# A 2x2 block product in seven multiplications inside a Fourier and feed-forward kernel

## The chip, the cores and the metric

One core of one Trainium2 chip. The time is the device time of one execution in microseconds, as the median of three runs. PE is the engine of the matrix products (PEld its weight loads), DVE, ACT and POOL are the vector, scalar and GpSimd engines, SP issues the transfers.

## The reference

```
x: (8, 3008, 256)
X  = rfft(x, axis=1)
Yr = Xr @ w_r - Xi @ w_i + b_r ;  Yi = Xr @ w_i + Xi @ w_r + b_i
Yr, Yi = sign(Y) * max(|Y| - 0.01, 0)
y  = irfft(Yr + i Yi)                        # (24064 tokens, 256)
h  = y @ w_in                                # 256 -> 2048
out = (h * clip(h + 3, 0, 6) / 6) @ w_out    # 2048 -> 256
```

All arrays are float32 except w_in and w_out, which arrive as float64.

## The kernel before

**Precision.** A float32 product is made of three single passes. Each operand is split into a high part and a low part (`split`, line 111: ACT copies the high part, DVE or POOL subtracts it for the low part), and `product` (line 116) sums low x high, high x low and high x high in PSUM. The weights of the feed-forward part are decoded on the chip from the 64-bit words (`decode`, line 135), in 16 bands of 512 columns: four of them with the buffers EARLY during the first batch's transform, the others with the buffers LATE during the first feed-forward units.

**Transform.** The length 3008 is 64 x 47, so the Fourier transform is one over n2 and one over n1. `stage1` (line 209) does the first for ten n1 at a time and writes to a scratch tensor in DRAM. `middle` (line 297) handles two k2 at a time, in three pieces: `s2` (over n1, with a split of the result), `s3` (the complex weights, the threshold, the rearrangement t, c, z, zhi, zlo) and `s5` (back over k1, to a second scratch tensor). `stage6` (line 413) goes back over k2 for one chunk of tokens, puts the features on the partitions and splits them into yhi and ylo, the low part on POOL.

**Feed-forward.** Each batch has seven chunks of tokens: four of 470 and three of 376 (MSPLIT). A unit is one chunk and 256 of the 2048 inner features, so a batch has 56 units and the whole run 448. `up` (line 451) makes 12 products into a PSUM tile ph of two banks (2 groups of 128 features x 2 halves of the 256 inputs x 3 passes), then on the whole tile: ACT relu(h + 3) into g, DVE min(g, 6) x h, ACT ghi, DVE glo. `down` (line 474) adds 12 products into po; it runs two units behind `up`.

**Order.** The main loop writes up(i), a slot, down(i - 2), a slot. The pieces of the transform of later batches lie in these slots: stage 2 to 5 of the next batch, stage 1 of the one after, stage 6 of the next chunk. The order of instructions on an engine follows this source order as far as operands are ready. Pools give two buffers to most tiles of the transform, three to ghi and glo; PSUM is ph (2 x 2 banks), po (2) and ps_a (2).

Of the kernel before, what the change touches and what calls it, by code (L numbers as in the profile page):

```python
# [37 lines left out]


def positions():  # L40
    """The order of the tokens in the result: by chunks, in each first n2 = q < 24, then n2 = 47 - q."""
    pos, order = sequence(), []
    for c, nj in enumerate(MSPLIT):
        n1 = 2 * sum(MSPLIT[:c]) + np.arange(2 * nj)
        order += [pos[n1, :NK].reshape(-1), pos[n1][:, N2 - np.arange(1, NK)].reshape(-1)]
    return np.concatenate(order)


def constants():
    """Matrices of the transforms, by shape alone."""  # L50
# [10 lines left out]
    # Sums of n2 = q and -q for the cosines, differences for the sines: rows (j, q), columns (c/s, j, k2),  # L61
    # and as the matrix is symmetric, rows (j, k2), columns (c/s, j, q) too.
# [4 lines left out]
    # rows (c/s, n1), columns k2, (re/im, k1)  # L67
# [5 lines left out]
    # rows (re/im, k1), columns (c/s, n1): for k2 = 0, then for the others  # L73
# [13 lines left out]
    f = lambda a, *s: np.ascontiguousarray(a.reshape(*s).astype(np.float32))  # noqa: E731  # L87
# [9 lines left out]
def spectral_ffn(ctx: ExitStack, tc: tile.TileContext, x, w_r, w_i, bias, w_in, w_out, f47, f64, g64, sgn, out):  # L97
    nc = tc.nc
    const = ctx.enter_context(tc.tile_pool(name="const", bufs=1))
    sb = ctx.enter_context(tc.tile_pool(name="sb", bufs=2))  # L100
    dram = ctx.enter_context(tc.tile_pool(name="dram", bufs=2, space=DRAM))
    ps_h = ctx.enter_context(tc.tile_pool(name="ps_h", bufs=2, space=PSUM))
    ps_o = ctx.enter_context(tc.tile_pool(name="ps_o", bufs=1, space=PSUM))
    ps_a = ctx.enter_context(tc.tile_pool(name="ps_a", bufs=2, space=PSUM))

    def room(wide=False):
        if wide:
            return ps_h.tile([P, 2, 512], F32, name="ph")[:, 0]
        return ps_a.tile([P, 512], F32, name="ps_a")

    def split(hi, lo, src, on=None):
        """src = hi + lo, each with the bits that one pass of a product carries."""
        nc.scalar.copy(out=hi, in_=src)  # L113
        (on or nc.vector).tensor_tensor(out=lo, in0=src, in1=hi.bitcast(F32), op=ALU.subtract)  # L114

    def product(ps, terms, start=True, stop=True):
        """The sum of (hi, lo)^T (hi, lo) over terms, into ps."""
        todo = [p for (ah, al), (bh, bl) in terms for p in ((al, bh), (ah, bl), (ah, bh))]
        for n, (a, b) in enumerate(todo):
            nc.tensor.matmul(out=ps, lhsT=a, rhs=b, start=start and n == 0, stop=stop and n == len(todo) - 1)  # L120

    def loaded(src, rows, cols, name, tag="g"):
        """A constant as its two parts."""
# [5 lines left out]

    depth = {"ghi": 3, "glo": 3, "ot": 1, "c": 1, "e": 1}  # L130

    def space(shape, dt, name, tag):
        return sb.tile(shape, dt, name=name, tag=tag, bufs=depth.get(tag, 2))

    def decode(src, hi, lo, cut, tags):
# [5 lines left out]
        e, m, r, mf, rf = (  # L141
            space([P, 2, 256], dt, t, tag) for t, dt, tag in zip("emrfg", (I32, I32, I32, F32, F32), tags[1:])
        )
# [5 lines left out]
        v.scalar_tensor_tensor(out=e, in0=high, scalar=-(1 << 31), in1=e, op0=ALU.bitwise_and, op1=ALU.bitwise_or)  # L149
# [3 lines left out]
        nc.gpsimd.tensor_tensor(out=cut(hi, 1), in0=mf, in1=base, op=ALU.mult)  # L153
# [3 lines left out]
        nc.gpsimd.tensor_tensor(out=cut(lo, 1), in0=rf, in1=base, op=ALU.mult)  # L157
# [8 lines left out]
    # brings the table of its functions in before the data is there  # L166
    nc.scalar.activation(out=three, in_=three, func=AF.Relu, scale=1.0)

    win_s = [const.tile([P, 2 * FF], F32R, name="w_in_" + t) for t in ("hi", "lo")]
    wout_s = [const.tile([P, NFT * D], F32R, name="w_out_" + t) for t in ("hi", "lo")]  # L170

    def in_band(f, early):
# [4 lines left out]
        decode(w_in, *win_s, cut, early)  # L177

    def out_band(f, early):
# [4 lines left out]
        decode(w_out, *wout_s, cut, early)  # L184

    EARLY = ("xin", "g", "yhi", "ylo", "qt", "ot")
    LATE = ("bt", "t", "Xhi", "zhi", "zlo", "Xlo")
# [19 lines left out]
    scr1, scr2, ys = {}, {}, {}  # L207

    def stage1(b):
        scr1[b] = dram.tile([2, N1, NK, D], F32, name="scr1")  # L210
        sets = [(n1, min(2 * J, N1 - n1)) for n1 in range(0, N1, 2 * J)]
        sets = sets[-1:] + sets[:-1]
        xins = {}

        def load(i):
            n1, n = sets[i]
            rows, w = (R47, 2 * D) if n == 2 * J else (n * NK, D)
            xins[i] = space([P, 2, 2 * D], F32, "xin", ("xin", "xin", "bt", "bt", "pt", "pt", "qt")[i] if b == 0 else "xin")
# [5 lines left out]
        if b == 0:  # L224
            shapes = [load(i) for i in range(len(sets))]
        for i, (n1, n) in enumerate(sets):
            rows, w = shapes[i] if b == 0 else load(i)
            xin = xins.pop(i)
            plus, minus = xin[:rows, 0, :w], xin[:rows, 1, :w]
            e = space([P, 2 * D], F32, "e", "t" if b == 0 else "e")[:rows, :w]  # L230
            (nc.vector if b == 0 else nc.gpsimd).tensor_tensor(out=e, in0=plus, in1=minus, op=ALU.add)
            (nc.vector if b == 0 and i % 2 else nc.gpsimd).tensor_tensor(out=plus, in0=plus, in1=minus, op=ALU.subtract)
            for c, src in enumerate((e, plus)):
                q = 2 * i + c
                tags = (("xhi", "xlo"), ("zhi", "zlo"), ("Xhi", "Xlo"))[q % 3 if b == 0 else 0]
                xs = [space([P, 2 * D], F32R, t, tag)[:rows, :w] for t, tag in zip(("xhi", "xlo"), tags)]
                split(*xs, src, nc.vector if b == 0 and (c == 0 or i % 2 == 0) else nc.gpsimd)
                ps = ps_o.tile([P, 2, 512], F32, name="po")[:, 0] if b == 1 and not ys else room(b == 0 and c)
                product(ps[:rows, :w], [([t[:rows, c * R47 : c * R47 + rows] for t in f47_s[:2]], xs)])
                a = space([P, 2 * D], F32, "a", ("a", "yhi", "ylo")[q % 3] if b == 0 else "a")[:rows, :w]  # L240
                if c and b == 0 and i in (0,2,4):
# [4 lines left out]
                nc.sync.dma_start(out=dst, in_=a.rearrange("p (g d) -> p g d", d=D))  # L246
                yield

    f64_s = const.tile([P, NK, P], F32, name="f64")
    sgn_s = const.tile([P, NK], F32, name="sgn")  # L250
    bias_s = const.tile([P, 2 * D], F32, name="bias")
    def load_f64(g):
        ks = slice(2 * g, 2 * g + 4)
        nc.sync.dma_start(out=f64_s[:, ks], in_=f64.rearrange("p (k c) -> p k c", c=P)[:, ks])

    w_m = [const.tile([P, 2 * D], F32R, name="w_m_" + t) for t in ("hi", "lo")]
    w_four = [[space([P, 2 * D], F32R, "w", tag) for _ in range(2)] for tag in ("ghi", "glo")]

    def weights():
        """w_i and -w_i, for batch 0; -(w_r + w_i) and w_i - w_r, for the others."""  # L260
# [18 lines left out]
    for i, _ in enumerate(stage1(0)):  # L279
        if i == 7:  # L280
            load_f64(0)
            r, k = [loaded(w, P, 2 * D, n) for w, n in ((w_r, "w_r"), (w_i, "w_i"))]
            nc.sync.dma_start(out=bias_s, in_=bias)
            nc.sync.dma_start(out=sgn_s, in_=sgn)
            g64_t = loaded(g64, P, 2 * P, "g64", "ot")
            todo = weights()
# [10 lines left out]
    def middle(b):  # L297
# [4 lines left out]
        bt, xs, zs, pt = {}, {}, {}, {}  # L302

        def s2(g):
            if g % 2 == 0:
                bt[g // 2] = sb.tile([P, 4, D], F32, name="bt")
                nc.sync.dma_start(out=bt[g // 2], in_=src[:, 2 * g : 2 * g + 4, :])
            if b == 0:
                if g and g % 2 == 0:
                    load_f64(g)  # L310
            ps = room(b == 0)
            psv = ps.rearrange("p (h r k c) -> p h r k c", h=2, r=2, k=2)
            for u in range(2):
                k2 = 2 * g + u
                for dh in range(2):
                    nc.tensor.matmul(  # L316
                        out=psv[:, dh, :, u, :],
                        lhsT=bt[g // 2][:, k2 % 4, dh * P : (dh + 1) * P],
                        rhs=f64_s[:, k2, :],
                        start=True,  # L320
                        stop=True,
                    )
            pv = ps.rearrange("p (h r c) -> p h r c", h=2, r=2)
# [218 lines left out]
    for i in range(len(units) + 2):  # L542
# [3 lines left out]
        if i >= 2:  # L546
            down(*units[i - 2])
# [50 lines left out]
```

## Time and profile before

| | |
|---|---|
| median of three runs | 2747.0 us (2746.18 to 2747.72) |
| span of the profiled execution | 2745.7 us |
| busy PE / PEld | 2678.2 us (98%) / 2495.5 us (91%), 15128 products |
| busy DVE | 1679.9 us (61%), 2439 instructions |
| busy ACT | 1329.7 us (48%), 1991 instructions |
| busy POOL | 473.4 us (17%), 349 instructions |
| mean granted TensorE clock | 0.986 |

The profile is of one execution, which has no time of its own beside its span from the first to the last instruction. Products on PE overlap, and the end of each is modelled: a busy share of PE, and the length of one product in its row, say little of what it costs. Better is the distance from one start to the next, which the chain of work that ended last shows in pieces. In rows of groups stand the count, then the busy time in all and the mean in ns of one, then the idle time of the engine before them with what ended it. In rows of a timeline stand the start, the length, engine, line, operation, and in brackets an idle time before it. Rows of windows give the busy time of PE, PEld, DVE, ACT and POOL in a stretch (with counts), the granted clock, the DMA share and GB/s.

### The profile page before, as it was taken

The numbers are of one execution on the slowest core, as the hardware profiler recorded it, in microseconds if no ns is written. First come the engines' busy times: TensorE is split into PE (matmuls) and PEld (weight loads), VectorE is DVE, ScalarE is ACT, GpSimd is POOL, SyncE is SP. The second block draws the span as 40 slices with busy tenths as digits, with TensorE's granted clock in tenths as the row PEclk, the third lists the DMA queues.
The fourth block names the chain that finished last, engine by engine and source line by source line (L and its number), as shares of the span: only waits on it lengthen the run. The fifth ranks groups of instructions, "written<-read, shape, count | busy, mean of one in ns | idle before, by whom it ended". The sixth has DMA issues, their size and how long they took to land.

```text
span 2745.7 us, 37533 instructions
## 1 busy us (share of the span) xinstructions
PE 2678.2 (98%) x15128; PEld 2495.5 (91%) x15128; DVE 1679.9 (61%) x2439; ACT 1329.7 (48%) x1991; POOL 473.4 (17%) x349
## 2 busy tenths in 40 slices
PE   6679999999999999999999999999999999999999
PEld 5668999999999899999999989998999999998899
DVE  7997666565656566566565566655656665654444
ACT  4345445544545445554554445545454444444443
POOL 3472211111111121111211121111110000000000
PEclk8889999999999999999999999999999999999999
DMA  7441212122121211211112111121212111010000
GB/s 210 148 132 59 64 54 84 48 61 64 33 86 45 66 52 42 82 59 49 51 49 82 54 55 57 40 85 47 69 40 68 29 43 42 21 43 26 20 14 18
DMA packets 94996, 163.90 MB, mean 60 GB/s; under 512 B 7279, under 2 KB 72551, under 8 KB 94823
## 3 DMA queue, kind: packets, MB, share of 16 engines
q1 hardware_dynamic: 94823, 161.51, 19.6%
q8 instruction: 119, 1.95, 0.3%
q14 instruction: 54, 0.44, 0.1%
HBM read 86.50 MB, written 74.97 MB: 59 GB/s over the span
## 4 chain that ended last, share of the span: by engine, by line
PE 92%; DVE 5%; DMA 1%; issue 1%; POOL 1%; ACT 0%; SPq 0%; DVEq 0%; POOLq 0%; ACTq 0%
PE po L120 38%; PE ph L120 38%; PE ps_a L120 11%; PE ps_a L428 3%; PE ps_a L316 3%; DVE z L371 1%; DMA xin<-in_x 1%; DVE e L146 0%; DVE m L151 0%; DVE zlo L380 0%; DVE e L149 0%; POOL w_out_hi L153 0%; DVE g L466 0%; DVE r L155 0%; DVE t L354 0%
## 5 line engine op out<-in xcount | busy, mean ns | idle before, releaser
L466 DVE SCALAR_TENSOR_TENSOR g<-g,ph 128x940 f32<-128x940 f32 (+1 forms) x448 | 470.0, 1049 | 605.6 <-ACT g L465 603.5
L465 ACT ACTIVATE g<-ph,three 128x940 f32<-128x940 f32 (+1 forms) x448 | 438.0, 978 | 598.5 <-PE ph L120 598.0
L114 DVE TENSOR_TENSOR glo<-g,ghi 128x940 fp32r<-128x940 f32 (+1 forms) x448 | 484.5, 1082 | 282.2 <-ACT ghi L113 278.9
L120 PE MATMUL ph<-yhi,w_in_lo 128*128 128x470 f32 (+1 forms) x1792 | 648.8, 362 | 7.1 <-POOL w_in_lo L157 7.1
L120 PE MATMUL po<-ghi,w_out_lo 128*128 128x470 f32 (+1 forms) x1792 | 654.6, 365 | 0.0
L120 PE MATMUL ph<-ylo,w_in_hi 128*128 128x470 f32 (+1 forms) x1792 | 643.8, 359 | 3.0 <-DVE ylo L114 3.0
L120 PE MATMUL ph<-yhi,w_in_hi 128*128 128x470 f32 (+1 forms) x1792 | 642.3, 358 | 0.0
L120 PE MATMUL po<-glo,w_out_hi 128*128 128x470 f32 (+1 forms) x1792 | 641.3, 358 | 0.0
L120 PE MATMUL po<-ghi,w_out_hi 128*128 128x470 f32 (+1 forms) x1792 | 640.3, 357 | 0.0
L113 ACT CAST ghi<-g 128x940 fp32r<-128x940 f32 (+1 forms) x448 | 408.5, 912 | 390.9 <-DVE g L466 390.7
L114 POOL TENSOR_TENSOR ylo<-y,yhi 128x470 fp32r<-128x470 f32 (+1 forms) x110 | 157.3, 1430 | 1239.2 <-ACT yhi L113 1239.2
L120 PEld LDWEIGHTS ph<-yhi,w_in_lo 128*128 128x128 f32 x1792 | 339.0, 189 | 32.4 <-POOL w_in_lo L157 7.5
L120 PEld LDWEIGHTS ph<-ylo,w_in_hi 128*128 128x128 f32 x1792 | 339.9, 190 | 27.3 <-DVE ylo L114 3.5
L120 PEld LDWEIGHTS ph<-yhi,w_in_hi 128*128 128x128 f32 x1792 | 338.4, 189 | 25.9
L120 PEld LDWEIGHTS po<-ghi,w_out_hi 128*128 128x128 f32 x1792 | 337.2, 188 | 26.6
L120 PEld LDWEIGHTS po<-ghi,w_out_lo 128*128 128x128 f32 x1792 | 338.3, 189 | 24.6 <-DVE ot L493 0.5
L120 PEld LDWEIGHTS po<-glo,w_out_hi 128*128 128x128 f32 x1792 | 338.5, 189 | 21.8
L379 ACT ACTIVATE zhi<-z,sgn 128x256 fp32r<-128x256 f32 x192 | 95.9, 507 | 213.8 <-DVE z L371 213.5
L371 DVE TENSOR_TENSOR z<-t,c 64x256 f32<-64x256 f32 x384 | 176.8, 460 | 7.1
L114 POOL TENSOR_TENSOR xlo<-xin,xhi 120x512 fp32r<-120x512 f32 (+1 forms) x52 | 66.7, 1284 | 550.1 <-ACT xhi L113 546.7
L428 PEld LDWEIGHTS ps_a<-f_all,qt 120*128 120x128 f32 (+1 forms) x896 | 118.1, 194 | 12.0 <-issue 8.9
L428 PE MATMUL ps_a<-f_all,qt 120*128 120x120 f32 (+1 forms) x896 | 118.0, 276 | 8.7 <-DMA qt<-scr 8.7
(119 smaller groups left out, 2859.2 us busy)
## 6 DMA issues: line engine op xcount, KB each, us to landing
bt<-scr SPq DMA_DIRECT2D x48, 512.0 KB, 3.8
scr<-pt SPq DMA_DIRECT2D x48, 512.0 KB, 2.6
xin<-in_x SPq DMA_DIRECT2D x48, 480.0 KB, 4.6
scr<-a SPq DMA_DIRECT2D x96, 240.0 KB, 2.5
qt<-scr SPq DMA_DIRECT2D x64, 240.0 KB, 3.6
out<-ot SPq DMA_DIRECT2D x32, 470.0 KB, 3.1
qt<-scr SPq DMA_DIRECT2D x48, 192.0 KB, 2.8
out<-ot SPq DMA_DIRECT2D x24, 376.0 KB, 4.1
```

Source lines behind the costliest of these rows:

```text
L113: nc.scalar.copy(out=hi, in_=src)
L114: (on or nc.vector).tensor_tensor(out=lo, in0=src, in1=hi.bitcast(F32), op=ALU.subtract)
L120: nc.tensor.matmul(out=ps, lhsT=a, rhs=b, start=start and n == 0, stop=stop and n == len(todo) - 1)
L316: nc.tensor.matmul(out=psv[:, dh, :, u, :], lhsT=bt[g // 2][:, k2 % 4, dh * P : (dh + 1) * P], rhs=f64_s[:, k2, :], start=True, stop=True,)
L371: nc.vector.tensor_tensor(out=z[ri * N1 : (ri + 1) * N1, u], in0=t[rows, ri], in1=c[rows, ri], op=ALU.subtract)
L379: nc.scalar.activation(out=zhi[:, u], in_=t[:, u], func=AF.Copy, scale=sc)
L428: nc.tensor.matmul(out=ps[:, cs * w + g * rows : cs * w + (g + 1) * rows], lhsT=qt[:rows, cs, g, dh * P : (dh + 1) * P], rhs=f47_s[2][:row ...
L465: nc.scalar.activation(out=g[:, :, :n], in_=ph[:, :, :n], func=AF.Relu, bias=three, scale=1.0)
L466: nc.vector.scalar_tensor_tensor(out=g[:, :, :n], in0=g[:, :, :n], scalar=6.0, in1=ph[:, :, :n], op0=ALU.min, op1=ALU.mult)
```

## The change

**Seven products.** The product onto FF is seen as a product of 2x2 blocks: the 512 tokens of a chunk in two halves of 256, the 256 inputs in two halves of 128, and a unit's 256 features in two groups of 128. Seven block products replace the eight. The combinations of the weights are made once, after decoding (`in_band`); those of the tokens once per chunk on POOL (`prepare`: four subtractions and seven splits). Each block product is three passes of 256 columns, so a unit's 12 products of 470 or 376 columns become 21 of 256. Products back onto D stay 12 a unit, of 512 columns.

**Phases.** A unit runs in four phases, spread over two steps of the loop and interleaved with those of the neighbours and four `down` parts. In one accumulator (pb) products are added on, and ACT copies it between them (p1, u2, u3, then the first half of h1); DVE adds products of other accumulators (pd, pc) to the copies. `gate` then does relu, min and product, high part and low part on each group of 512 columns, from SBUF.

**Chunks.** All 24064 tokens are one stream of 47 chunks of 512 (376 units). `segment` replaces `stage6`: ten n1 (470 tokens) at a time, written into the raw tiles of one or two chunks, cut at the border.

**Buffers.** Most tiles of the transform have one buffer instead of two (batch 0 borrows others), so `middle` now runs s5, s3, s2 in this order; bt and pt hold two k2 instead of four, and the matrices f64 are loaded again for every batch. PSUM is pb (2 banks), pd, pc, po0, po1 and ps_a (2).

```diff
-    sb = ctx.enter_context(tc.tile_pool(name="sb", bufs=2))
+    sb = ctx.enter_context(tc.tile_pool(name="sb", bufs=1))
+    depth = {"gs": 4, "yb": 9, "raw": 2, "h0": 3, "h1": 2, "r": 3, "ot": 2, "p1": 2, "u2": 2, "bt": 2, "f64": 2}
...
+        mf, rf, base = decode(w_in, cut, tags)
+        nc.gpsimd.tensor_tensor(out=mf, in0=mf, in1=rf, op=ALU.add)
+        nc.gpsimd.tensor_tensor(out=mf, in0=mf, in1=base, op=ALU.mult)
+        ...
+        split(hi[:, :2], lo[:, :2], mf[:, :, :P])
+        split(hi[:, 2], lo[:, 2], a22)
+        split(hi[:, 3:], lo[:, 3:], s)
...
-    LATE = ("bt", "t", "Xhi", "zhi", "zlo", "Xlo")
+    EARLY = ("raw", "yb", "yb", "yb", "yb", "yb", "ot")
+    LATE = ("xin", "bt", "t", "z", "zhi", "zlo", "pt")
...
+    def prepare(c):
+        y = raw.pop(c)
+        b11, b12, b21, b22 = y[:, 0, :H], y[:, 0, H:], y[:, 1, :H], y[:, 1, H:]
+        s = space([P, 4, H], F32, "T")
+        for to, p, q in ((0, b12, b11), (1, b22, s[:, 0]), (2, b22, b12), (3, b21, s[:, 1])):
+            nc.gpsimd.tensor_tensor(out=s[:, to], in0=p, in1=q, op=ALU.subtract)
+        yield
+        for n, src in ((2, b21), (1, b11), (6, s[:, 1]), (7, s[:, 2]), (5, s[:, 0]), (4, s[:, 3]), (3, b22)):
+            t = space([P, 2, H], F32R, "yb")
+            split(t[:, 0], t[:, 1], src, nc.gpsimd)
+            yb[c, n] = (t[:, 0], t[:, 1])
+            yield
...
+    def kept(i, n, ps):                      # ACT
+        t = keep[i, n] = space([P, H], F32, n)
+        nc.scalar.copy(out=t, in_=ps)
+    def added(i, u, half, ps, n):            # DVE
+        nc.vector.tensor_tensor(out=hs[i, u][:, half * H : (half + 1) * H], in0=ps, in1=keep.pop((i, n)), op=ALU.add)
+    def phase_a(i):
+        ...
+        block(i, 2, pd, True)
+        block(i, 1, pb, True)
+        kept(i, "p1", pb)
+        added(i, 0, 0, pd, "p1")
+    def phase_b(i):
+        block(i, 6, ps_of[i], False)
+        kept(i, "u2", ps_of[i])
+    def phase_c(i):
+        ...
+        block(i, 7, ps_of[i], False)
+        block(i, 5, pc, True)
+        kept(i, "u3", ps_of[i])
+        added(i, 1, 1, pc, "u3")
+    def phase_d(i):
+        ...
+        block(i, 4, pb, False)
+        block(i, 3, pc, False)
+        nc.scalar.copy(out=hs[i, 1][:, :H], in_=pb)
+        added(i, 0, 1, pc, "u2")
...
-            up(*units[i])
-            fill(2 * i)
...
-            down(*units[i - 2])
...
-            fill(2 * i + 1)
+            phase_a(i)
+        gated(i - 2)                         # high and low parts
+        fill(4 * i)
+            down(i - 3, 0, 0)
+            phase_c(i - 1)
+        fill(4 * i + 1)
+            down(i - 3, 0, 1)
+            phase_b(i)
+        fill(4 * i + 2)
+            down(i - 2, 1, 0)
+            phase_d(i - 1)
+            gates[i - 1] = gate(i - 1)
+            gated(i - 1)                     # relu, min and product
+        fill(4 * i + 3)
+            down(i - 2, 1, 1)
```

More of the change, by code (lines that the diff above doesn't have):

```diff
@@ L128, in loaded, with run, decode @@
         return hi, lo, st[:rows, :cols]
[L130 to L135, printed above, removed]
+    def run(g):
+        for _ in g:
+            pass
+    nf = NFT // 2
+    three = const.tile([P, 1], F32, name="three")
+    nc.vector.memset(three, 3.0)
+    nc.scalar.activation(out=three, in_=three, func=AF.Relu, scale=1.0)
+    win_s = [const.tile([P, nf, 7, P], F32R, name="w_in_" + t) for t in ("hi", "lo")]
+    wout_s = [const.tile([P, NFT * D], F32R, name="w_out_" + t) for t in ("hi", "lo")]
+    def decode(src, cut, tags):
         st = space([P, 2, 256, 2], I32, "st", tags[0])
@@ L156, in decode, with in_band @@
         nc.scalar.activation(out=rf, in_=r, func=AF.Copy, scale=2.0**-42)
[L157 to L172 removed]
+        return mf, rf, base
+    def in_band(f, tags):
         def cut(t, words):
@@ new lines, in spectral_ffn, with block @@
+    units = [(c, f) for c in range(NC) for f in range(nf)]
+    hs, ps_of, keep, gs, pos = {}, {}, {}, {}, {}
+    def block(i, n, ps, start):
+        c, f = units[i]
+        product(ps, [(tuple(t[:, f, WEIGHT[n]] for t in win_s), yb[c, n])], start=start, more=True)
+    def kept(i, n, ps):
[3 more added lines that the diff above has]
+        nc.vector.tensor_tensor(out=hs[i, u][:, half * H : (half + 1) * H], in0=ps, in1=keep.pop((i, n)), op=ALU.add)
@@ new lines, in down @@
+    def down(i, u, dh):
+        c, f = units[i]
+        ft = 2 * f + u
+        first, last = f == 0 and u == 1, f == nf - 1 and u == 0
+        if first:
+            pos[dh] = ps_o.tile([P, 512], F32, name=f"po{dh}")
+        g = gs[i, u]
+        product(
+            pos[dh],
+            [(part(wout_s, slice(ft * D + dh * P, ft * D + (dh + 1) * P)), (g[:, 0], g[:, 1]))],
+            start=first,
+            stop=last,
+        )
+        if dh:
+            gs.pop((i, u))
+        if last:
+            ot = space([P, T], F32, "ot")
+            if dh:
+                nc.vector.tensor_scalar(out=ot, in0=pos[dh], scalar1=1.0 / 6.0, scalar2=None, op0=ALU.mult)
+            else:
+                nc.scalar.mul(out=ot, in_=pos[dh], mul=1.0 / 6.0)
+            nc.sync.dma_start(out=out[dh * P : (dh + 1) * P, c * T : (c + 1) * T], in_=ot)
@@ L504, in spectral_ffn @@
     run(mid)
[L505 to L511 removed]
+    for k in range(2):
+        run(segment(0, k))
+    run(prepare(0))
     slots = {}
[L513 to L533 removed]
@@ L535, in spectral_ffn, with lay @@
-    for q in range(14 - early):
-        slots.setdefault(2 + q, []).append(nxt)
+    def lay(g, n, first, last):
+        q = -1
+        for i in range(n):
+            q = max(q + 1, int(4 * (first + (last - first) * i / n)))
+            while q in taken:
+                q += 1
+            taken.add(q)
+            slots.setdefault(q, []).append(g)
+    taken = set()
+    per = S / 64
+    begin = {}
+    for b in reversed(range(B)):
+        for k in reversed(range(len(SEGS))):
+            first = 8 * ((b * S + SEGS[k][0] * N2) // T)
+            begin[b, k] = min([first - 8.5, *([begin[b, k + 1] - 3] if (b, k + 1) in begin else [])])
+            if k + 1 == len(SEGS) and (b + 1, 0) in begin:
+                begin[b, k] = min(begin[b, k], begin[b + 1, 0] - 3)
@@ new lines, in spectral_ffn @@
+    for c in range(1, NC):
+        g = prepare(c)
+        for n in range(8):
+            slots.setdefault(max(0, 4 * (8 * c - 5) + 2 * n), []).append(g)
+    rest = 14 - early
+    lay(nxt, rest + 1, 1, 8)
+    for b in range(B):
+        for k in range(len(SEGS)):
+            if (b, k) not in ((0, 0), (0, 1)):
+                lay(segment(b, k), 3, max(0, begin[b, k]), max(3, begin[b, k] + 3))
+        if b:
+            lay(middle(b), 3 * (NK // 2) + 1, max(9, per * (b - 1) - 14), begin[b, 0] - 1.5)
+        if b > 1:
+            lay(stage1(b), 15, max(9, per * (b - 2) - 10), per * (b - 1) - 16)
```

337 lines of the change are left out of this document (171 added, 166 removed).

## The prediction

> **What bounds the kernel now.** I read the page from the top, then the chain of waits, then stretches of exactly one batch, then the chain in order of time, then single groups by shape.
>
> ```profile
> span 2745.7 us, 37533 instructions
> PE   6679999999999999999999999999999999999999
> PEclk8889999999999999999999999999999999999999
> PE 92%; DVE 5%; DMA 1%; issue 1%; POOL 1%; ACT 0%; SPq 0%; DVEq 0%; POOLq 0%; ACTq 0%
> ```
>
> ```profile
> core 0: us, PE busy (x) PEld busy (x) DVE busy (x) ACT busy (x) POOL busy (x), PEclk, DMA share, GB/s
> 126.00:216.00 90.00, 65.30 (x277) 54.87 (x278) 81.29 (x109) 43.32 (x69) 61.38 (x39) 0.80 0.48 136
> 600.00:928.00 328.00, 328.00 (x1877) 307.33 (x1876) 197.75 (x291) 164.13 (x247) 54.52 (x42) 1.00 0.19 58
> ```
>
> After the third slice PE never rests, at clock 1.00, and holds 92% of the chain. A batch takes 328 us; in it DVE is busy 60%, ACT 50%, POOL 17%. Before about 216 us DVE and POOL (81.3 and 61.4 us of 90) set the pace, decoding weights. The span is 1.3 us below the 2747.0 us median.
>
> A busy matmul row overlaps the next, so prices come from the chain in order of time, whose pieces end where the next starts:
>
> ```profile
> 1003.15 2.55 PE ph L120 x12
> 2405.44 2.06 PE ph L120 x12
> 1021.17 0.71 PE ps_a L120 x3
> 1024.43 2.15 PE ps_a L120 x18
> 1015.19 0.89 PE ps_a L316 x8
> 1005.71 0.86 PE ps_a L428 x8
> ```
>
> Twelve products of 470 columns take 2.55 us (0.2125 each), of 376 columns 2.06 (0.1717), three of 512 columns on 120 rows 0.71 (0.237), and eighteen of 256 columns 2.15 (0.119). The line through 470 and 376 gives 0.1168 at 256: the small shape carries 2 ns extra, no more. It gives 0.2307 at 512.
>
> **The change on PE.** Before, a batch has 32 units of 24 products at 470 and 24 units of 24 at 376: 32x24x0.2125 + 24x24x0.1717 = 262.1 us. With the pieces s2, s3 and s5 of each pair of k2 (0.89 + 2.15 + six at 0.119 = 3.75, x12 = 45), stage 1 (14x0.71 = 9.9) and stage 6 (112 products at 0.1075 = 12) that is 329, against 328 in the window, so the prices hold. After, a batch is 47 units of 512 tokens (376 in all), each with 21 products at 256 and 12 at 512: 2.50 + 2.77 = 5.27 us, x47 = 247.6. At 0.237 for 512 it is 251.0; I take the line, whose rows are the same 128-row products. Segments need 100 products instead of 112: -1.3. Gain 15.8 us a batch (12.4 by the other end), x8 = **-126** (-99). So a batch would need 312 us of PE.
>
> **The other engines in a batch.**
>
> ```profile
> L114 DVE TENSOR_TENSOR glo<-g,ghi 128x940 fp32r<-128x940 f32 x256 | 300.5, 1174 | 163.6 <-ACT ghi L113 161.1
> L466 DVE SCALAR_TENSOR_TENSOR g<-g,ph 128x940 f32<-128x940 f32 x256 | 289.9, 1132 | 367.6 <-ACT g L465 365.8
> L114 DVE TENSOR_TENSOR glo<-g,ghi 128x752 fp32r<-128x752 f32 x192 | 184.0, 958 | 118.5 <-ACT ghi L113 117.8
> L466 DVE SCALAR_TENSOR_TENSOR g<-g,ph 128x752 f32<-128x752 f32 x192 | 180.1, 938 | 238.0 <-ACT g L465 237.7
> L114 DVE TENSOR_TENSOR w_m_lo<-cst,w_m_hi 128x512 fp32r<-128x512 f32 x1 | 0.7, 691 | 0.0
> L331 DVE TENSOR_TENSOR xi<-ps_a,xi 128x256 f32<-128x256 f32 x84 | 34.8, 415 | 0.0
> L328 ACT COPY xi<-ps_a 128x256 f32<-128x256 f32 x84 | 31.1, 370 | 27.5 <-PE ps_a L316 27.5
> L113 ACT CAST w_r_hi<-cst 128x512 fp32r<-128x512 f32 x1 | 0.6, 631 | 0.0
> L114 POOL TENSOR_TENSOR xlo<-e,xhi 96x256 fp32r<-96x256 f32 x7 | 5.2, 739 | 9.3 <-ACT xhi L113 9.3
> L114 POOL TENSOR_TENSOR ylo<-y,yhi 128x470 fp32r<-128x470 f32 x62 | 93.1, 1502 | 672.2 <-ACT yhi L113 672.2
> ```
>
> DVE loses two instructions a unit, 32x2.31 + 24x1.90 = 119 us a batch; it gains per unit three additions of 256 out of PSUM (0.415) and four passes of 512 (0.69), 4.0 us, x47 = 188, and about 6 us because a segment's writes are cut at chunk borders. 197 - 119 + 194 = 272 of 312 us: 87%. ACT has four copies of 256 (0.37) and four passes of 512 (0.63) a unit, 4.0 us against 2.0 before, and ends near 250 of 312. POOL swaps 14 ylo passes (about 20 us) for 11 passes of 256 per chunk (0.74, 5.9 chunks: 48 us): 83 us. None is over 312 alone. But in a unit everything now hangs together: one accumulator is read by ACT between additions of products (p1, u2, u3), the next product waits for that copy, and the second accumulator waits for DVE.
>
> How long a reader waits for a product shows here:
>
> ```profile
> 1005.33 0.37 PE L120 MATMUL ph<-yhi,w_in_hi 128*128 128x470 f32 x1
> 1005.80 1.04 ACT L465 ACTIVATE g<-ph,three 128x940 f32<-128x940 f32 x1 [2.02 <-PE ph L120]
> ```
>
> The reader starts 0.47 us after the last product, 0.26 more than that product's 0.21 of PE time. I walked one unit by these rows. The u3 copy ends about 3.4 us into the unit, the addition that reads it about 4.1, and the product that then adds into the same bank is due at 4.23. So an empty unit just fits, with 0.1 us to spare. A unit that carries an s3 piece doesn't:
>
> ```profile
> 1043.52 0.69 DVE L361 TENSOR_TENSOR t<-ps_a,bias 128x512 f32<-128x512 f32 x1 [2.25 <-PE ps_a L120]
> 1044.13 0.93 DVE L466 SCALAR_TENSOR_TENSOR g<-g,ph 128x752 f32<-128x752 f32 x1
> 1044.98 0.68 DVE L364 TENSOR_TENSOR t<-ps_a,t 128x512 f32<-128x512 f32 x1
> 1045.69 0.43 DVE L365 TENSOR_SCALAR c<-t 128x512 f32<-128x512 f32 x1
> 1046.89 1.73 DVE L371 TENSOR_TENSOR z<-t,c 64x256 f32<-64x256 f32 x4
> 1048.65 1.03 DVE L380 SCALAR_TENSOR_TENSOR zlo<-z,sgn,zhi 128x256 fp32r<-128x256 f32 x2
> ```
>
> Without the pass of g these are 4.6 us of DVE; with the unit's 4.0 that is 8.6 against 5.27 + 2.15 = 7.4 us of PE, 1.2 short. Queued behind them on DVE are the additions that free PSUM and the low parts that the products back onto D wait for. Products of a later unit can be brought forward (above, a pass of g stands between two instructions of one s3: the order on an engine follows readiness, not the source alone). Bounds: nothing, or 1.2 us for each of 84 such pieces = 101. In the middle, with no row nearer to either end: **+50**.
>
> Single transform buffers: a piece must finish before the next of its kind. There are 37 pieces in 47 units, so one every 8.4 us of PE; the s3 chain above lasts 6.2. I cost it at nothing on that cover; were the cover short by 1 us, 84 groups would cost 84. The 24 more DMA issues a batch on SP (bt, f64 and pt for two k2 instead of four) take under 0.4 us each of an otherwise idle queue; a bt issue that waits for its buffer holds up the qt and output issues behind it, which are due units later. On POOL the chunk's passes queue among those of stage 1; the blocks of the next chunk get their buffers about one unit (5.3 us) before they are read, against 0.37 + 0.74 us for copy and low part. Nothing, on that cover; 1 us at each of 47 borders without it.
>
> **The start.** Until the weights are decoded, DVE and POOL pay for everything, and POOL and DVE take turns:
>
> ```profile
> 160.34 1.34 POOL L232 TENSOR_TENSOR xin<-xin 120x512 f32<-120x512 f32 x1
> 160.47 2.21 DVE L114 TENSOR_TENSOR glo<-g,ghi 128x940 fp32r<-128x940 f32 x1
> 168.65 1.12 DVE L114 TENSOR_TENSOR glo<-g,ghi 128x940 fp32r<-128x940 f32 x1
> 195.53 1.12 DVE L466 SCALAR_TENSOR_TENSOR g<-g,ph 128x940 f32<-128x940 f32 x1
> 195.74 1.27 POOL L153 TENSOR_TENSOR w_in_hi<-f,e 128x512 fp32r<-128x512 f32 x1 [2.97 <-DVE e L149]
> st<-in_w_in SPq DMA_DIRECT2D x8, 512.0 KB, 4.6
> ```
>
> The pass glo takes 1.12 us alone at 168.65, but 2.21 at 160.47, where it ends 1.0 us after POOL's pass: it stood until POOL was done. The pass of g, with one input in PSUM, keeps its 1.12 at 195.53 with POOL's pass beside it. Decoding reads SBUF alone, so both engines' additions count as one here: low parts of the seven blocks, 1.4 us for each of 8 bands (11); four more POOL passes a band, at most 0.74 each (24); 11 POOL passes before the first unit (8); 1.7 us more DVE in each of the first eight units (14). Together 57 if all of it is serial, 25 if only DVE's counts. The late bands also share single buffers where they had two, so that a band's load (4.6 us to landing) may stand bare, up to 12 x 4.6 = 55, less what units fill. I take **+45**; range 10 to 100. The end has the last unit's gate behind four smaller steps: **+3**.
>
> **Sum.** 2745.7 - 126 + 50 + 45 + 3 = 2717.7, and with the 1.3 us to the median **2719 us**.
>
> A rule of the Trainium skill speaks against the change. "TensorE: Matmul & The Clock Gate", section "The mechanism" of the part on packing small matmuls, says that a weight load overlaps running products only when it goes to other rows of the array. By that rule each of 33 loads a unit would add its own time. The trace disagrees here: 256-column products start every 0.119 us with a full 128x128 load before each.
>
> **Rivals.**
> (A) All hidden: the later products brought forward absorb s3, and the start costs only 15. 2747 - 126 + 15 + 3 = 2639. For it: 13% of DVE's time is still free. Against it: 0.1 us of slack.
> (B) Slower: POOL holds DVE up, and the pair becomes the bound. DVE's 272 plus POOL's 83 is 355 a batch if never side by side; additions out of PSUM can run beside POOL, as the pass of g did. With 60 of the 83 held, a batch takes 332: +4x8 + 45 = 2824. It decides from about 50 of the 83: then 322 a batch uses up what the start leaves of the gain. For it: the row at 160 us. Against it: in the steady batches glo rises only from 1.12 to 1.17. "GPSIMD Engine Reference" of the Trainium skill, section "1. Specifications", says that POOL contends with DVE instructions that have two SBUF inputs; the rows at 160 us agree.
> (C) Slower by the chain within each unit: a product waits for a copy in every unit, not only in those with s3. 0.3 us x 376 = 113 in place of 50: 2782. It decides from 0.2 us a unit. Against it: the walk just fits.
> (D) Seven products cost no less than eight, since 33 loads must pass where 24 did:
>
> ```profile
> L120 PEld LDWEIGHTS ph<-yhi,w_in_hi 128*128 128x128 f32 x1792 | 338.4, 189 | 25.9
> ```
>
> At 0.189 a small product, 7896 x 0.07 = +553: 3270. The row of eighteen in 2.15 us is against it.
>
> **Chances.** Forecast 0.41 (own range 2680 to 2745), A 0.22, B 0.18, C 0.17, D 0.02. About 0.2% (5.5 us) is what a measurement of this kernel can tell from no change. The forecast's upper edge and C's lower one reach into that. Faster 0.60, same 0.07, slower 0.33. The range reaches from just below A to C and most of B: 2632 to 2815.
>
> **What would show it.** Right: matmuls of 256 columns start every 0.12 us; about 312 to 318 us between the same points of two batches; DVE busy 85 to 90%; PE waits of about 0.5 us in units with s3, for u3, u2 or gs; full PE from about 260 us instead of 216. Wrong: PE waiting on additions or copies in all units (C); DVE passes of 512 well over 0.69 us with POOL beside them (B); a start longer by more than 100 us.

## The result and the profile after

The changed kernel takes 2926.8 us (median; 2918.7 to 2932.8), the kernel before 2747.4 on the same chip: 1.0652 times as long (95% interval 1.0629 to 1.0674), 180 us slower where 28 us faster was forecast.

The page of the changed kernel:

```profile
span 2930.5 us, 45975 instructions
PE 2690.4 (92%) x16720; PEld 2391.2 (82%) x16720; DVE 2280.0 (78%) x4358; ACT 1955.6 (67%) x4335; POOL 780.7 (27%) x788
...
PE   5665798999999999999999999999999999999999
...
PEclk8875799999999999999999999999999999999999
...
PE 64%; DVE 21%; issue 5%; POOL 5%; ACT 4%; DMA 1%; SPq 0%; DVEq 0%; POOLq 0%; ACTq 0%
```

The chain of waits, 92% PE before, is 64% PE, 21% DVE and 5% POOL now. PE's slices are below nine tenths six times in the first seven (5665798), where that held for the first three (667). The same two stretches as before:

```profile
core 0: us, PE busy (x) PEld busy (x) DVE busy (x) ACT busy (x) POOL busy (x), PEclk, DMA share, GB/s
126.00:216.00 90.00, 57.02 (x278) 49.39 (x279) 37.87 (x87) 31.75 (x67) 27.74 (x30) 0.75 0.28 77
600.00:928.00 328.00, 315.83 (x2024) 281.90 (x2023) 271.76 (x511) 232.50 (x521) 89.00 (x88) 0.99 0.21 62
```

At the start no engine is full: DVE is busy 38 of 90 us where it was 81. In the steady part PE rests 12 of 328 us although DVE is busy only 83%.

How much of the loss lies where is read from the copy of a chunk's last output (ACT, tile ot). Its first row starts at 341.2 us, and the fifth and the 29th chunk end here:

```profile
609.55 0.60 ACT L609 ACTIVATE ot<-po 128x512 f32<-128x512 f32 x1 [0.33 <-PE po L131]
...
2020.55 0.60 ACT L609 ACTIVATE ot<-po 128x512 f32<-128x512 f32 x1 [0.65 <-PE po L131]
```

That is 1411.0 / 24 = **58.8 us a chunk** (some expectations below say 58.4) with all parts of the transform beside it, called "a chunk" below; a batch is 5.875 chunks. The forecast's 312 us a batch would be 53.1, the 328 before 55.8. The first four chunks (2048 tokens) are done at 555.9 us; before, 2048 tokens were done at about 397 (between the outputs at 376.6 and 422.9). From there to the last output it takes 2370 us, before 2344. So of 185 us between the two profiled spans 159 came in the first four chunks and 26 in the rest, where some 115 should have been won.

### The profile page after: what moved, and what is told of

It is laid out like the page before. It is cut to its first block, busy times and chain, and to the rows that moved or that the text cites. A ratio compares the mean times of both kernels' runs of the same rounds, so it can differ in the third digit from the quotient of the medians.

```text
span 2930.5 us, 45975 instructions
## 1 busy us (share of the span) xinstructions
PE 2690.4 (92%) x16720; PEld 2391.2 (82%) x16720; DVE 2280.0 (78%) x4358; ACT 1955.6 (67%) x4335; POOL 780.7 (27%) x788
## 3 DMA queue, kind: packets, MB, share of 16 engines
q8 instruction: 131, 2.15, 0.3%
## 4 chain that ended last, share of the span: by engine, by line
PE 64%; DVE 21%; issue 5%; POOL 5%; ACT 4%; DMA 1%; SPq 0%; DVEq 0%; POOLq 0%; ACTq 0%
PE po L131 27%; PE pb L131 13%; PE ps_a L131 9%; PE pc L131 7%; DVE z L403 4%; PE pd L131 3%; DVE gs L586 3%; DVE zlo L411 3%; PE ps_a L472 3%; PE ps_a L346 2%; DVE r L575 2%; DVE h L536 2%; DVE r L583 2%; POOL xlo L125 1%; DVE t L396 1%
## 5 line engine op out<-in xcount | busy, mean ns | idle before, releaser
L131 PE MATMUL po<-gs,w_out_hi 128*128 128x512 f32 x3008 | 971.4, 404 | 15.9 <-DVE gs L586 15.6
L131 PEld LDWEIGHTS po<-gs,w_out_hi 128*128 128x128 f32 x3008 | 570.8, 192 | 95.5 <-DVE gs L586 28.9
L131 PE MATMUL po<-gs,w_out_lo 128*128 128x512 f32 x1504 | 618.9, 412 | 25.8 <-ACT gs L581 15.5
L131 PE MATMUL pb<-yb,w_in_hi 128*128 128x256 f32 x3008 | 610.8, 284 | 1.0 <-POOL yb L125 1.0
L586 DVE TENSOR_TENSOR gs<-r,gs 128x512 fp32r<-128x512 f32 x752 | 559.2, 769 | 27.3 <-ACT gs L581 22.5
L573 ACT ACTIVATE r<-h,three 128x512 f32<-128x512 f32 x752 | 516.9, 719 | 59.4 <-DVE h L536 50.1
L131 PEld LDWEIGHTS pb<-yb,w_in_hi 128*128 128x128 f32 x3008 | 472.9, 193 | 51.7 <-POOL yb L125 1.4
L536 DVE TENSOR_TENSOR h<-pc,u 128x256 f32<-128x256 f32 x752 | 315.6, 420 | 247.6 <-PE pc L131 233.1
L581 ACT CAST gs<-r 128x512 fp32r<-128x512 f32 x752 | 451.8, 623 | 78.0 <-DVE r L575 57.8
L131 PE MATMUL pb<-yb,w_in_lo 128*128 128x256 f32 x1504 | 432.3, 287 | 8.6 <-ACT u L533 4.0
L575 DVE SCALAR_TENSOR_TENSOR r<-r,h 128x512 f32<-128x512 f32 x376 | 300.5, 799 | 91.1 <-ACT r L573 89.6
L583 DVE SCALAR_TENSOR_TENSOR r<-r,h 128x512 f32<-128x512 f32 x376 | 286.5, 762 | 12.1 <-ACT r L573 11.0
```

What stands on the lines that cost most here:

```text
L536: nc.vector.tensor_tensor(out=hs[i, u][:, half * H : (half + 1) * H], in0=ps, in1=keep.pop((i, n)), op=ALU.add)
L573: nc.scalar.activation(out=r[u], in_=hs[i, u], func=AF.Relu, bias=three, scale=1.0)
L575: nc.vector.scalar_tensor_tensor(out=r[u], in0=r[u], scalar=6.0, in1=hs.pop((i, u)), op0=ALU.min, op1=ALU.mult)
L581: nc.scalar.copy(out=t[:, 0], in_=r[u])
L583: nc.vector.scalar_tensor_tensor(out=r[0], in0=r[0], scalar=6.0, in1=hs.pop((i, 0)), op0=ALU.min, op1=ALU.mult)
L586: nc.vector.tensor_tensor(out=t[:, 1], in0=r[u], in1=t[:, 0].bitcast(F32), op=ALU.subtract)
```

## The first reading, and the experiments

PE's prices were as forecast:

```profile
600.13 0.36 PE pb L131 x3
600.49 0.70 PE po L131 x3
...
629.95 2.15 PE ps_a L131 x18
```

Three 256-column products in 0.36 us, three of 512 in 0.70, s3 in 2.15. So the loss is in waits. The stretch behind that s3 piece (DVE, ACT, POOL and PE; other rows left out):

```profile
636.18 3.06 DVE L411 SCALAR_TENSOR_TENSOR zlo<-z,sgn,zhi 128x256 fp32r<-128x256 f32 x2
...
636.23 1.29 POOL L261 TENSOR_TENSOR e<-xin 120x512 f32<-120x512 f32 x1 [13.53 <-DVE z L403]
...
637.60 1.36 POOL L262 TENSOR_TENSOR xin<-xin 120x512 f32<-120x512 f32 x1
...
638.92 1.46 POOL L125 TENSOR_TENSOR xlo<-e,xhi 120x512 fp32r<-120x512 f32 x1
639.16 0.41 DVE L536 TENSOR_TENSOR h<-pc,u 128x256 f32<-128x256 f32 x1
639.50 1.42 DVE L575 SCALAR_TENSOR_TENSOR r<-r,h 128x512 f32<-128x512 f32 x1
...
639.63 0.38 PE L131 MATMUL pc<-yb,w_in_lo 128*128 128x256 f32 x1 [0.50 <-DVE h L536]
```

The two zlo passes, 1.03 us together before, take 3.06 while POOL makes e and the difference. The addition of h, queued behind them, starts at 639.16, and PE waits for it. That addition reads PSUM and keeps its 0.41 beside POOL's xlo; r, which reads SBUF twice, takes 1.42 in place of 0.69. POOL's e had waited 13.5 us for DVE's z, and this is the rule:

```profile
POOL e L261 <- DVE z L403: 431.1, 45, 29.8
...
DVE h L536 <- PE pc L131: 233.5, 242, 3.2
```

Since the change, stage 1's e and s3's c share one buffer (tag "e"). So POOL starts just when z frees it, which is when DVE comes to zlo. PE's own waits between 600 and 1958 us are 66 us in all; these are the longest (us in all, times, longest of one):

```profile
PE pc L131 <- DVE h L536: 18.2, 16, 3.3
PE po L131 <- ACT gs L581: 14.3, 9, 3.0
PE ps_a L131 <- POOL xlo L125: 12.9, 9, 1.7
PE po L131 <- DVE gs L586: 8.1, 15, 1.2
PE ps_a L131 <- ACT xhi L124: 8.0, 8, 2.1
```

They are of two kinds. 41 us end with h or gs: DVE's additions, and the parts that ACT and DVE make from DVE's r, which come late when a DVE pass before them is held. The other 21 end with stage 1's halves: there PE waits for POOL's own late work (xlo, and e, from which ACT makes xhi), since e had waited for the shared buffer. The chunk's blocks yb, which POOL also makes, are not among the waits. (The stretch loses 111 us, 4.8 in each of 23 chunks, against the runs in which POOL is empty; the granted clock of 0.98 against 1.00 there may be some 27 of it, an estimate, and what the rest beside the waits is no view shows.)

My theory then: this sharing, and single buffers at the start. Rivals: the chain within each unit, or DVE simply too full. Chunks and times of all runs:

| run | median us | first chunk done | four chunks done | a chunk |
|---|---|---|---|---|
| changed kernel | 2926.8 | 341.2 | 555.9 | 58.8 |
| c in a buffer of its own | 2845.7 | 335.1 | 543.5 | 56.0 |
| two sets for late bands | 2906.2 | 311.8 | 528.8 | 58.8 |
| batch 0 in the old order | 2904.7 | 304.6 | 527.7 | 58.9 |
| eight products | 2892.1 | 307.9 | 524.2 | 57.8 |
| the three edits | 2780.4 | 277.6 | 479.4 | 55.9 |
| c apart, no low parts on POOL | 2782.0 | 322.1 | 518.2 | 54.9 |
| c apart, POOL's passes on DVE | 2744.2 | 318.0 | 516.4 | 54.0 |
| three edits, more early bands | 2785.5 | 281.9 | 482.9 | 56.1 |
| three edits, POOL's passes on DVE | 2689.8 | 262.4 | 460.3 | 54.0 |
| POOL's passes on DVE alone | 2755.9 | 319.9 | 519.0 | 54.2 |
| three edits, POOL's and the bands' passes on DVE | 2671.7 | 241.6 | 440.7 | 54.0 |
| three edits, POOL's passes on DVE, eight products | 2763.9 | 238.3 | 436.8 | 56.1 |
| before, POOL's passes on DVE | 2739.4 | | | |
| only stage 1's passes on DVE | 2812.5 | 323.0 | 524.8 | 55.5 |
| only the chunks' passes on DVE | 2871.8 | 327.1 | 539.8 | 57.7 |

### c in a buffer of its own

```diff
-            c = space([P, 2, D], F32, "c", tag(g, "e", "h1"))
+            c = space([P, 2, D], F32, "c", tag(g, "c", "h1"))
```

> The changed kernel with one edit: the tile c of s3 has a buffer of its own, where it shared one with stage 1's e. Theory (sharing): POOL's addition e waits for DVE's z (45 times, 431 us), so POOL's passes start just as DVE comes to zlo, which then takes 1.5 us in place of 0.5. Apart, the pass zlo returns to about 0.5 us, the wait of e for z is gone, a chunk with all transforms takes 55 to 56 us in place of 58.4, and the time is 2840 to 2880 in place of 2927. Rival (the chain within each unit, or DVE simply too full): zlo gets shorter, but POOL then holds other DVE passes, and a chunk stays within 0.7 us of 58.4; 2900 to 2930.

Measured: 2845.7 us, 81 less (ratio to before 1.0365, 1.0348 to 1.0383). Groups of DVE between 600 and 1958 us, the changed kernel and then this run:

```profile
L586 DVE TENSOR_TENSOR gs<-r,gs 128x512 fp32r<-128x512 f32 x370 | 281.7, 785 | 13.8 <-ACT gs L581 11.7
...
L411 DVE SCALAR_TENSOR_TENSOR zlo<-z,sgn,zhi 128x256 fp32r<-128x256 f32 x94 | 84.3, 910 | 1.1
```

```profile
L586 DVE TENSOR_TENSOR gs<-r,gs 128x512 fp32r<-128x512 f32 x389 | 295.7, 784 | 10.3 <-ACT gs L581 8.0
...
L411 DVE SCALAR_TENSOR_TENSOR zlo<-z,sgn,zhi 128x256 fp32r<-128x256 f32 x100 | 52.3, 537 | 1.2
```

zlo falls from 910 to 537 ns, and PE's waits for stage 1's halves are gone: its waits in the stretch fall from 66 to 32 us. So the 81 us hold both kinds of wait. But gs stays at 784 in place of 684 with POOL empty (shown below): POOL now holds other passes, and 56.0 is still above 53.1.

### Two sets of buffers for the late bands

```diff
-    LATE = ("xin", "bt", "t", "z", "zhi", "zlo", "pt")
+    LATE = ("xin", "bt", "z", "zhi", None, None, "zlo"), ("st", "bt", "t", "pt", None, None, "Xhi")
```

(None: the conversion writes its own input. The sets alternate.)

> The changed kernel with one edit: the twelve late bands of weights alternate between two sets of buffers, with a second tile for the load, as each band converts in place. Theory (the start is serial through single buffers): the first chunk is done at 280 to 300 us in place of 341, and the time is 40 to 55 lower, 2870 to 2890. Rival (the start is set by the work of POOL and DVE on each band, whatever the buffers): first chunk at 330 or later, 2915 to 2930.

2906.2 us: 21 less, half of what was expected. The first chunk is done 29 us earlier, so the bands did wait for their buffers, but not only for them.

### Batch 0 in the old order

```diff
+            steps = [(s5, g - 2), (s3, g - 1), (s2, g)]
+            for step, k in steps[::-1] if b == 0 else steps:
```

> The changed kernel with one edit: in batch 0 the pieces run s2, s3, s5 as before the change, where they ran s5, s3, s2. In batch 0 the tiles alternate between two tags, so this needs no buffer. Theory (batch 0's pieces wait for each other in this order): the first product onto FF is at 155 to 165 us in place of 185, and the time is 20 to 30 lower. Rival (the pieces wait for the shared buffer of e and c and for the weights' decoding): within 8 us of the changed kernel.

2904.7 us: 22 less. The first product onto FF starts at 149.4 us in place of 185.3, more than expected; 8 of these 36 us are lost again by the fourth chunk.

### Eight products in the changed structure

```diff
-    def block(i, n, ps, start):
+    def group(i, u, ps):
+        c, f = units[i]
+        hs[i, u] = ps
+        product(ps, [(tuple(t[:, f, 2 * u + dh] for t in win_s), yb[c, dh]) for dh in range(2)])
```

> The changed kernel with the product onto FF by eight block products again, 12 matmuls of 512 columns a unit, with no combinations of weights or tokens; chunks of 512, the single stream, the single transform buffers, the order of the loop and the four gs and nine yb buffers stay. PE's price a unit is 24 x 0.2307 = 5.54 us, 0.27 more than with seven. Theory (the loss is in the single buffers and the start, the seven products only make it worse): still slower than before the change, 2800 to 2860: the first chunk at 310 to 330 us, a chunk with all transforms 56 to 57. Rival (the loss comes with the seven products: DVE's load and the chain within a unit): all is back, 2735 to 2770, the first chunk near 250 us and a chunk of 56.

2892.1 us, above both ranges. So most of the loss is not in the seven products: with eight the same structure loses 145 us to the kernel before. A chunk takes 57.8 against PE's 56.0; with seven 58.8 against 53.1. Seven suffer more from the same waits.

### The three edits together

> The changed kernel with three edits: c shares its buffer with pt in place of e, the late bands have two sets of buffers, batch 0 runs s2, s3, s5. Theory (three separate waits, one in the steady batches and two in a row at the start): the gains add up, 81 + 21 + 22: about 2805 us; first product onto FF at 150, first chunk done at 275 to 285, a chunk with all transforms 56. Rival (the two at the start hide one another, as one engine is behind both): 2825 to 2845, first chunk at 295 or later.

2780.4 us (1.012, 1.0105 to 1.0135): 146 less, more than the 124 of the single edits and below the range of the theory. So the waits at the start were separate ones. By the fourth chunk the three together bring 76 us where the single edits bring 68; that each had hidden a part of the others would explain it, but no run shows that.

### c apart, POOL's low parts left out

```diff
-            split(t[:, 0], t[:, 1], src, nc.gpsimd)
-            yb[c, n] = (t[:, 0], t[:, 1])
+            nc.scalar.copy(out=t[:, 0], in_=src)
+            yb[c, n] = (t[:, 0], t[:, 0])
```

> c in a buffer of its own, and POOL's low parts left out from batch 1 on (stage 1) and for all chunks (the high part stands in for the low one, so the products and their number stay): of POOL's 93 us a batch about 52 go, nothing is added elsewhere. The result then lacks those low parts. Theory (POOL holds DVE): DVE's passes of 512 columns come down toward 0.69, and a chunk with all transforms takes 54 to 54.8 us in place of 56.0; 2800 to 2825. Rival (what is left is the chain within each unit and DVE's own load): 55.5 or more; 2830 to 2846.

2782.0 us, 64 less than with c apart alone; POOL's busy time in 600 to 928 goes from 91 to 41 us, a chunk from 56.0 to 54.9, gs to 734 ns. This is the theory that POOL holds DVE; the time is below its range, the chunk just above it.

### c apart, POOL's passes on DVE

```diff
-            nc.gpsimd.tensor_tensor(out=s[:, to], in0=p, in1=q, op=ALU.subtract)
+            nc.vector.tensor_tensor(out=s[:, to], in0=p, in1=q, op=ALU.subtract)
...
-            split(t[:, 0], t[:, 1], src, nc.gpsimd)
+            split(t[:, 0], t[:, 1], src)
```

(and likewise e, the difference and xlo of stage 1 from batch 1 on)

> c in a buffer of its own, and POOL's passes of stage 1 (from batch 1 on) and of the chunks moved to DVE, where a pass of 512 takes 0.69 in place of 1.4 us. POOL is then empty after the start, DVE has some 46 us a batch more and loses what POOL held it (about 25): near 295 of 312. Theory (POOL holds DVE): a chunk takes 55 to 56 us, no worse than the 56.0 with POOL. Rival (DVE's own load is the bound, POOL hardly matters): 57.5 or more, the time 2880 or more.

2744.2 us: 101 less than with c apart, with a chunk of 54.0, better than the 55 to 56 expected, and level with the kernel before (0.9984, 0.9975 to 0.9994). Windows of the run with c apart, then of this one, then this one's gs:

```profile
600.00:928.00 328.00, 318.29 (x2059) 286.48 (x2058) 272.95 (x516) 238.07 (x535) 91.13 (x91) 0.99 0.21 62
```

```profile
600.00:928.00 328.00, 327.66 (x2159) 298.25 (x2158) 293.54 (x636) 250.24 (x562) 0.00 (x0) 1.00 0.22 65
```

```profile
L586 DVE TENSOR_TENSOR gs<-r,gs 128x512 fp32r<-128x512 f32 x403 | 268.6, 684 | 3.9 <-ACT gs L581 3.0
```

This decides against "DVE is too full". DVE takes over 91 us of POOL's time and gets only 21 us busier (its passes are shorter, and it is held up no more); at 89% PE hardly waits (3 us between 600 and 1958), at 83% with POOL beside it PE waited 32. None of those 32 us was a wait for POOL itself, so here it is the hold on DVE that costs.

### More bands early

```diff
-        if i % 9 == 7:
+        if i % 5 == 4:
```

(seven bands beside batch 0's transform in place of four; the three edits stand)

> The three edits, and seven bands instead of four decoded beside batch 0's transform, where DVE is busy 27 of 64 us. Theory (batch 0's transform waits for latencies, not for an engine, so bands fit into it): the first product 5 to 12 us later than with the three edits, the first chunk done 15 to 25 earlier, 2785 to 2800. Rival (each band costs the same wherever it stands): within 8 us of the three edits.

2785.5 us, 5 more than the three edits: the first product starts 10.5 us later, the first chunk is done 4 us later. The time lies in both ranges; the first chunk, later and not 15 to 25 us earlier, decides for the rival: a band costs about the same wherever it stands.

### The three edits and POOL's passes on DVE

> The three edits (c with pt, two sets for the late bands, batch 0 in the order s2, s3, s5) and POOL's passes of stage 1 and of the chunks on DVE. Theory (waits of the start and POOL's hold on DVE are separate): the fourth chunk done near 455 us (479 with the three alone, less the 27 that moving POOL's passes brought there), then the 2225 us of the run with POOL's passes on DVE: 2675 to 2695. Rival (with DVE near 95% in the first chunks, the start gives nothing more): 2705 to 2725.

2689.8 us, **2.1% faster than the kernel before** (0.979, 0.9776 to 0.9805). POOL works only while weights are decoded, and PE is full from the fifth slice on:

```profile
span 2690.0 us, 45549 instructions
...
PE   5767999999999999999999999999999999999999
...
POOL 3134000000000000000000000000000000000000
```

From 600 to 1958 us PE's waits are 3 us in all, and the chunk is (1809.43 - 512.93) / 24 = 54.0:

```profile
512.93 0.60 ACT L607 ACTIVATE ot<-po 128x512 f32<-128x512 f32 x1 [0.33 <-PE po L131]
...
1809.43 0.60 ACT L607 ACTIVATE ot<-po 128x512 f32<-128x512 f32 x1 [1.24 <-PE po L131]
```

### POOL's passes on DVE alone

> The changed kernel with POOL's passes of stage 1 and of the chunks moved to DVE, and e and c still in one buffer. Theory (the sharing costs only because it makes POOL start while DVE runs zlo): with e on DVE's own queue the shared buffer costs next to nothing, 2740 to 2765, a chunk near 54.2. Rival (the sharing has a price of its own, as stage 1 waits for s3): 2790 or more, a chunk of 55.5 or more.

2755.9 us (1.0033, 1.0021 to 1.0044). This edit alone takes back 171 of the 180 us. With c apart as well it is 12 less. So the shared buffer, which I had taken for the cause, costs little by itself: it set the moment at which POOL came.

### The bands' passes on DVE too

```diff
-            nc.gpsimd.tensor_tensor(out=s[:, to], in0=a, in1=b, op=op)
+            nc.vector.tensor_tensor(out=s[:, to], in0=a, in1=b, op=op)
```

(and the other five lines of the bands on POOL)

> The run with the three edits and POOL's passes on DVE, and the bands' passes on POOL (six for w_in, two for w_out) on DVE as well. Theory (POOL holds DVE at the start too): POOL's some 50 us of the stretch 190 to 300 become 25 on DVE, first chunk done 8 to 20 us earlier. Rival (DVE and POOL work side by side there, and DVE becomes the bound): first chunk 5 to 25 us later.

2671.7 us (0.9727, 0.9712 to 0.9741), the best of all: the first chunk done at 241.6 us in place of 262.4. POOL held DVE at the start too, as rows of the run before this edit show:

```profile
191.71 0.43 DVE L177 TENSOR_SCALAR e<-st 128x512 int32<-128x512 int32 x1
...
201.00 1.27 POOL L196 TENSOR_TENSOR m<-m,e 128x512 f32<-128x512 f32 x1
201.07 1.49 DVE L177 TENSOR_SCALAR e<-st 128x512 int32<-128x512 int32 x1 [2.37 <-POOL w_out_lo L218]
```

This pass has a single input, in SBUF, and still took 1.49 us in place of 0.43: not only passes with two SBUF inputs stood. But the edit also replaces POOL's passes by shorter ones in a band's chain of steps, and no run separates the two.

The page of the run with the bands' passes on DVE:

```profile
span 2668.9 us, 45516 instructions
...
PE   6768999999999999999999999999999999999999
...
PEclk8879999999999999999999999999999999999999
```

### Eight products in the mended structure

> The run with the three edits and POOL's passes on DVE, with eight block products in place of seven (12 matmuls of 512 columns a unit, no combinations). Theory (in a structure that no longer waits, seven products bring their price on PE): a chunk with all transforms at PE's price, 329 / 5.875 = 56.0 us, the rest after the fourth chunk near 2318, the time 2755 to 2780, some 80 to 95 above the same with seven. Rival (seven products give back what they save on PE): within 25 us of seven.

2763.9 us, 74 more than the same with seven, a little less than the 80 to 95 expected. The chunk is (1837.46 - 491.69) / 24 = 56.1 in place of 54.0:

```profile
491.69 0.60 ACT L568 ACTIVATE ot<-po 128x512 f32<-128x512 f32 x1 [1.48 <-PE po L131]
...
1837.46 0.60 ACT L568 ACTIVATE ot<-po 128x512 f32<-128x512 f32 x1 [1.18 <-PE po L131]
```

In the 344 units after the fourth chunk seven products save 99 us (2225.1 against 2324.6), where PE's prices give 344 x 0.27 = 93; 24 are lost again by the fourth chunk, in which the combinations of the weights are made.

### The kernel before with POOL's passes on DVE

> The kernel before the change with POOL's passes of stage 1 (from batch 1 on) and of stage 6 (ylo) moved to DVE. Theory (POOL's hold costs only where DVE's results are awaited; before, PE never waited in the steady batches and DVE was busy 60%): no gain in the steady batches, 2738 to 2752. Rival (POOL cost the kernel before something too, so that its loss is not the change's): 2730 or less.

2739.4 us (0.9962, 0.9949 to 0.9975). Its steady batch is full of PE as ever, with DVE 21 us busier than the 197.75 of before:

```profile
600.00:928.00 328.00, 328.00 (x1876) 307.08 (x1876) 219.20 (x332) 164.44 (x247) 0.00 (x0) 1.00 0.20 58
```

The 10 us come at the start (first output at 207.3 in place of 219.6 us). So POOL's hold cost the old kernel nothing once it was running: the steady loss is the change's own.

### Which of POOL's passes

```diff
-            (nc.vector if b == 0 else nc.gpsimd).tensor_tensor(out=e, in0=plus, in1=minus, op=ALU.add)
+            nc.vector.tensor_tensor(out=e, in0=plus, in1=minus, op=ALU.add)
```

(with the difference and xlo: only stage 1's passes; then only the eleven passes a chunk)

> The changed kernel with only stage 1's passes (e, the difference, xlo) moved from POOL to DVE; the eleven passes a chunk stay on POOL, e and c stay in one buffer. Theory (stage 1's passes do most of it, since they start when z frees the buffer, with zlo next on DVE): 2790 to 2825. Rival (the eleven passes a chunk do most of it): 2850 or more.

> The changed kernel with only the eleven passes a chunk moved from POOL to DVE; stage 1's stay on POOL, with e and c in one buffer. Theory (stage 1's passes do most of it): 2845 to 2885, a chunk with all transforms 57 or more. Rival (the eleven passes a chunk do most of it): 2825 or less.

2812.5 and 2871.8 us: stage 1's passes cost 114, the chunks' 55, together 169 of the 171. Per batch stage 1's are fewer (28 of some 1.4 us against 65 of 0.8 to 1.0), so each costs more. Two reasons are in the rows above: they start just when DVE comes to zlo, and PE waits for their results. With the chunks' passes alone moved, PE's waits for xlo and xhi stay (24 of 57 us between 600 and 1958).

## Why the prediction was wrong

**The products: nearly right.** 256 columns start every 0.12 us and 512 every 0.233, with a weight load before each; rival D is out. Without waits a batch takes 54.0 x 5.875 = 317 us, against the 312 taken; the other price of 512 columns (0.237) would have given 315.6, and the gain of 11 us a batch is nearer to its 12.4 than to the 15.8 taken. From the fourth chunk to the last output the run with the three edits and an empty POOL needs 2225 us, the kernel before 2344: 119 won, where 115 were forecast for these 43 chunks. That the two agree is partly luck: 99 of the 119 are the seven products, by the run with eight (2324.6), and 20 the rest of the structure, perhaps transform work already done in the first four chunks; no run separates these 20 further.

**The stalls: the step that failed.** I set +50 between 0 and 101, from DVE's own 1.2 us too many in units with s3. With POOL's passes moved, PE hardly waits although DVE does that work and more: the later products brought forward do absorb it, as rival A said. In its place stand POOL's passes, for which the term had nothing: 2370 - 2225 = 145 us after the first four chunks, 141 of them by moving these passes alone. Of the 145, 69 are the hold on DVE: with c apart PE never waits for POOL itself, and moving the passes then brings 69. The other 76 go with the shared buffer of e and c. In them the hold on zlo and PE's waits for stage 1's late halves are mixed (21 of 66 us of PE's waits are of the second kind), and no run separates them. The prediction had looked at POOL's blocks for the chunk, for which PE indeed does not wait, and not at stage 1's halves. I had the row that shows the hold (glo at 2.21 in place of 1.12 us) and the rival (B, 0.18), but weighed it by the steady part of before, where glo rose only from 1.12 to 1.17. That was the wrong measure in two ways. There, half of DVE's long passes read PSUM, and the products that wait for glo come two units later; after, r and gs both read SBUF twice, and the walk through one unit had shown 0.1 us of slack. And B was priced as a sum of loads, as if the pair had to be full: 332 us a batch. It took no full engine. What counts is lateness in front of an addition that PE waits for (1.1 us in the mean of 16 waits, 3.3 at most); the time was 58.8 x 5.875 = 345 us a batch with DVE at 83%.

The Trainium skill's "SBUF — State Buffer", section "SBUF: two separate sides", says of the port pair that DVE and GpSimd share that it is "an **exclusive lock**, not a bandwidth split", which goes to whoever starts first for a whole instruction, and that a DVE pass needs it when it has two SBUF inputs. The runs agree that the pass stands: zlo and r took about as long as POOL's pass beside them, the addition out of PSUM kept its 0.41 us. Who starts first they do not show: the record of zlo begins 0.05 us before that of POOL's e, and zlo stood. "Perfetto Trace Analysis" of the Trainium skill, section "Optimizing GPSIMD Operations", prefers other engines where possible; here that was worth 171 us.

**The start: mis-sized.** +45 (10 to 100) was forecast, some +170 came: 159 by the fourth chunk, and the 11 that the products should have won on those 2048 tokens. I had added up work; the runs show waits in a row, for buffers and for the order of the pieces. Alone, the order s5, s3, s2 cost 36 us before the first product and the single buffers of the late bands 29 by the first chunk. One after the other, by the fourth chunk: the three edits bring 76 us (555.9 to 479.4), POOL's passes on DVE 19, the bands' 20. Then four chunks are done at 440.7 us, still 43 later than before the change. The seven products with their combinations account for some 24 (436.8 against 460.3 with eight and seven products, the bands still on POOL); batch 1's transform, now laid within units 9 to 30, may be a part of the rest, which no run separates.

**Single transform buffers at nothing** was wrong by their indirect effect: with POOL empty the single buffers cost next to nothing in the steady part (PE waits 3 us in 1358, and a chunk is 54.2 us with e and c in one buffer, 54.0 with c apart), but the shared tile of e and c timed POOL's passes, and batch 0 and the bands waited in a row. C (a chain in every unit) has its sign in none of the runs with POOL empty.

In sum 2930.5 - 2745.7 = 185 is: -119 by the products and the structure after the first four chunks (forecast -126 in all), +145 stalls (+50), +159 in the first four chunks (+45). The +3 for the end is told apart by no run.

## What to carry to other kernels

Before moving work to POOL, list DVE's passes that read only SBUF (those with two inputs, and here also one-input passes of the decoding) and ask who waits for what is queued behind them: each can stand for a whole POOL pass, and one pass of POOL here was twice as long as the same on DVE. Ask also whether PE waits for POOL's results themselves. A busy share tells nothing of this: an engine at 89% that is never held can be better than one at 83% that is. When two tiles of different engines share a buffer, ask also at which moment the one that waits will start.

## What was not expected of the hardware

- POOL's passes of 120x512 from SBUF took 1.31 to 1.48 us in the mean of a row (changed kernel, 600 to 1958 us), the same on DVE 0.68 to 0.69 with POOL empty. With c apart, moving 91 us of POOL's time to DVE made DVE 21 us busier in 328, and the time 101 us shorter.
- The granted clock was lower where PE had holes: 0.66 between 190 and 300 us in the changed kernel, where PE was busy 65 of 110 us, and 0.92 with the bands on DVE, where it was busy 92.
